# Infini-attention and a Fourier mixer on one core: three steps of the woven stage later in SyncE's order, and one pair of row loads into other buffers

## The chip, the cores and the metric

The kernel runs on one core of one Trainium2 chip. Its engines are TensorE (PE in the profile), VectorE (DVE), ScalarE (ACT), GpSimd (POOL) and SyncE (SP), which here does nothing but issue DMAs. The metric is device time in microseconds (us), lower is better, as the median of several runs.

## What is computed

Two independent layers, whose outputs are joined along the features. A is attention with a compressive memory: 2048 tokens, 576 features, 32 heads of 18, four segments of 512. B is a discrete Fourier transform over the features and then over the tokens, real part only.

```python
def _A_ref(x, wq, wk, wv, wo, beta):
    # q, k, v: x @ w, split into 32 heads of 18 and N = 4 segments of L = 512
    for s in range(N):
        qs, ks, vs = q[:, :, s], k[:, :, s], v[:, :, s]
        logits = jnp.einsum("bhqd,bhkd->bhqk", qs, ks) * scale + mask
        p = _softmax(logits, axis=-1)
        a_dot = jnp.einsum("bhqk,bhkd->bhqd", p, vs)
        pq = phi(qs)
        num = jnp.einsum("bhld,bhde->bhle", pq, M)
        den = jnp.einsum("bhld,bhd->bhl", pq, z)[..., None] + 1e-6
        outs.append(g * (num / den) + (1.0 - g) * a_dot)
        M = M + jnp.einsum("bhld,bhle->bhde", phi(ks), vs)
        z = z + jnp.einsum("bhld->bhd", phi(ks))
    return o @ wo                                   # o: outs, heads joined again

def _B_ref(x, dft_seq_re, dft_seq_im, dft_hid_re, dft_hid_im):
    a = jnp.einsum("bsd,ed->bse", x, dft_hid_re)
    b = jnp.einsum("bsd,ed->bse", x, dft_hid_im)
    return jnp.einsum("ts,bse->bte", dft_seq_re, a) - jnp.einsum("ts,bse->bte", dft_seq_im, b)
```

Everything is float32; the kernel splits operands into a high and a low part and adds up products of the parts.

## The kernel before

**Three stages.** The first projects q, k and v segment by segment, looks up the memory, and leaves q and k (`qd`, `kd`, as bf16 pieces in six slots of a row), the values (`vd`) and the memory's part of the output (`amd`) in DRAM. The second, here called the woven stage, runs the softmax attention of all heads and both passes of B at once. The third, the output stage, multiplies the attention output (`od` in DRAM) with `wo`.

**The weave.** `attention()` is a generator over head pairs p = 0 to 67, with eight slots a pair. The main loop takes one slot, calls `tick()`, and then takes pieces of `dense()`, the work of B, until B has had its share. Each engine runs its own instructions in the order in which they are written down by this walk, and SP issues its DMAs in that order too. `later(n, f)` puts f off to the n-th tick from now, so eight ticks are one pair. A step due at a tick is written down before the pieces of `dense()` that follow the slot.

**What attention loads.** Four heads form a group G, so a group is two pairs. `stack_load(G)` puts two DMAs off by one and two ticks: the group's rows of `kd` into `ks_bufs`, and of `qd` into `qs_bufs`; there are four such buffers. Group 0 is loaded in the first stage, group 1 at p = 0, group (p + 3) // 2 in slot 5 of every odd p, so the third group (G = 2) at p = 1. Its first scores are computed in slot 1 of p = 4. `value_load(G)` loads the values of a group into one of two `vst` buffers; the first product with group 0's values (`pv`) comes in slot 2 of p = 4. `copy_parts(s, n)` copies some pieces of q or k rows from one slot of `qd` or `kd` to another, which the stacks of the later groups read; the copies for segment 2, n = 8 to 15, are written down at the odd pairs 1 to 15, those of segment 3 at the even pairs from 4. They serve groups from G = 20 on.

**Maxima.** In slot 4 of an odd p, `maxima(G)` (L1015 to L1018, four small operations on POOL) cuts the row maxima of a group; in slot 1 of the next pair `maxima_transpose` (L1022) transposes them on PE, ACT copies them (L1024), and one tick later two small DMAs `qs<-mt` put them into the stack.

**What B loads.** B works through a list of tiles, `CHUNKS`. For the first pass these are 16 tiles of the transposed input (`xtT`, 320 KB) and then tiles of the sequence matrix (`cT`, 256 KB). `c_load(n)` loads tile n into one of four `craw` buffers; `hidden(0, n)` asks for tile n + 4 when it begins, and in its middle has tile n + 2 cut (`c_cut`): ACT makes the high part (L451, L453), POOL the low part one tick later (L456, L458). `hidden` itself is L628 to L634. The tiles 0 to 4 are loaded in the first stage.

**Output stage.** Sixteen token tiles are worked on as eight pairs (n, n + 8) in steps n = 0 to 7. A step has seven products (`p1` to `p7`), of which `p4` and `p3` belong to the pair before; they end in the stores of that pair. `left(n + 1)` prepares the next pair from its rows during step n: POOL and DVE add and subtract, ACT and DVE cut (L833 to L853). `o_load` loads the rows of a token tile from `od`, 320 KB. Pair 0 goes into `qs3`/`ks3`, pair 1 into one buffer each of the tags `phi` and `plo` (two buffers each, used by attention until its end), pairs 2 and 3 into the four `craw` buffers at the end of B, and pairs 4 to 7 into `craw` again at the start of steps 2 to 5. The intermediate tiles `u` rotate through ten buffers, four a step.

**The last rows.** After the last product of attention, `pv_out`, `turn_out` (L1118: transposed by DVE, then stored to `od`) and `turn_tails` (L1130: DVE transposes the last eight features of four groups, DMA to `odt`, DMA from `odt` twice into the fifth part of `od`) follow one another through `later`; their ticks fall into the steps 0 and 1. The rows of tiles 12 to 15 need them. Before a row load, `while due: tick()` writes down everything that is still put off.

Of the kernel before, what the change touches and what calls it, by code (L numbers as in the profile page):

```python
# [12 lines left out]
F32 = mybir.dt.float32  # L13
# [10 lines left out]
P = 128  # L24
# [16 lines left out]
def infini_attention_and_fnet(ctx: ExitStack, tc: tile.TileContext, xT, wqk, w8, wv, wo, beta, xtT, cT, hT, out):  # L41
# [46 lines left out]
    def later(n, fn, *a):  # L88
        due.setdefault(clock[0] + n, []).append((fn, a))
# [112 lines left out]
    for i in range(2):  # L202
        kn.append(tuple(sk.tile([P, D], F32R, name=f"kn{n}{i}") for n in "hl"))
        t = sk.tile([P, 2, H, 19], F32R, name=f"vn{i}")
# [3 lines left out]
    for i in range(3):  # L208
        t = sb.tile([P, H, 55], BF16, name=f"vs{i}")
# [277 lines left out]
    def stack_load(G):  # L487
        if G < NG:
            s, g8 = divmod(G, 8)
            rows = slice(g8 * 72, g8 * 72 + 72)  # L490
            for n, (buf, src) in enumerate(((ks_bufs, kd), (qs_bufs, qd))):
                later(1 + n, dma, buf[G % 4][:NPAIR], src[s][rows].rearrange("(h d) c t -> (d c) h t", d=DH))

    def value_load(G):
        if G < NG:
            s, g8 = divmod(G, 8)
            VS[G] = sa.tile([P, 4, 220], BF16, name="vst", bufs=2)
            dma(VS[G], vd[s][:, :, g8])

    for s in range(NSEG):  # L500
# [8 lines left out]
        for n, m in enumerate((0, 1, 2, 3, 8, 4, 5, 6, 7)):  # L509
# [12 lines left out]
            if not more and n == 4:  # L522
                p1k.close()
                sr = ctx.enter_context(tc.tile_pool(name="sb2r", bufs=1, side="right", reuse_waits="tile"))
# [39 lines left out]
    def bank(name, shape, dtype, tag):  # L564
        turns[tag] ^= 1
        return ps.tile(shape, dtype, name=name, tag=f"{tag}{turns[tag]}", bufs=1)
# [117 lines left out]
    def o_load(t, tile_of):  # L684
        s, a = divmod(t, 4)
        o = tile_of()
        dma(o, od[s][:, a * P:a * P + P].rearrange("c p x -> p c x"))
        O[t] = o

    def o_pair(n):  # L690
        for t in (n, n + 8):
            o_load(t, lambda: sr.tile([P, 5, P], F32, name="craw", bufs=4))

    PLAN = {}

    def right_operands():
        raw, late = {}, {}

        def at(p, slot, fn, *a):
            PLAN.setdefault(8 * p + slot, []).append((fn, a))  # L700
# [102 lines left out]
        for t in (0, 8):  # L803
            at(66, 4, o_load, t, lambda t=t: sq.tile([P, 4, 256], F32, name="oraw", tag="qs3" if t else "ks3").rearrange(
                "p a x -> p (a x)")[:, :5 * P].rearrange("p (k x) -> p k x", k=5))
        for t, tag in ((1, "phi"), (9, "plo")):
            at(67, 4, o_load, t, lambda tag=tag: sa.tile([P, 5, P], F32, name="oraw", tag=tag, bufs=2))
        prepare = []
        at(67, 2, lambda: prepare.append(left(0)))
        for n in range(6):  # L810
# [45 lines left out]
    def seventh(o, n, x, w, first=False, tail=None):  # L856
        hi, lo = LEFT[n][x]
        terms = []
        for c in range(2):
            wh, wl = WO[w, c]  # L860
            terms += [(hi[:, c], wl), (hi[:, c], wh), (lo[:, c], wh)]
        if tail:
            terms += [(LEFT[n][tail[0]], m) for m in TAIL[tail[1]]]
        for i, (a, b) in enumerate(terms):
            pe.matmul(o, a, b, start=first and i == 0, stop=True, skip_group_check=True)  # L865
# [6 lines left out]
    def output_stage(second):  # L872
        C, Z, U = slice(0, 288), slice(288, 576), {}

        def p1(n):
            u = U[n] = [sb.tile([P, 576], F32, name="u", tag="ab", bufs=10) for _ in range(4)]
            u += [bank("s", [P, L], F32, "s")[:, :288], bank("t", [P, L], F32, "t")[:, :288],
                  ps.tile([P, 288], F32, name="d", bufs=3)]
            seventh(u[4], n, "A11", "B11", True)
            yield  # L880
            act.activation(u[0][:, C], u[4], AF.Copy)

        def p6(n):
            u = U[n]
            seventh(u[5], n, "S2", "T2", True)
            yield
            dve.tensor_tensor(u[0][:, Z], u[5], u[0][:, C], OP.add)

        def p4(n):
            u = U[n]  # L890
            seventh(u[5], n, "A22", "T4", tail=(2, 0))
            yield
            dve.tensor_tensor(u[3][:, C], u[5], u[0][:, C], OP.add)
            store(n + 8, u[3], slice(0, D))

        def p5(n):
            seventh(U[n][6], n, "S1", "T1", True)
            yield

        def p3(n):  # L900
            u = U[n]
            seventh(u[6], n, "S4", "B22", tail=(1, 2))
            yield
            dve.tensor_tensor(u[2][:, Z], u[6], u[0][:, Z], OP.add)
            store(n, u[2], Z if n == 7 else slice(0, D), n == 7)

        def p7(n):
            u = U[n]
            seventh(u[5], n, "S3", "T3", tail=(2, 2))
            yield  # L910
            dve.tensor_tensor(u[1][:, C], u[5], u[0][:, C], OP.add)
            dve.tensor_tensor(u[3][:, Z], u[6], u[1][:, C], OP.add)

        def p2(n):
            u = U[n]
            seventh(u[4], n, "A12", "B21", tail=(1, 1))
            yield
            act.activation(u[2][:, C], u[4], AF.Copy)
            if n == 7:
                store(n, u[2], C)  # L920

        for n in range(8):
            todo = [(p1, n), (p6, n), (p4, n - 1), (p5, n), (p3, n - 1), (p7, n), (p2, n)]
            if n == 7:
                todo += [(p4, n), (p3, n)]
            if 2 <= n < 6:
                while due:
                    tick()
                o_pair(n + 2)
            prepare = second if n == 0 else left(n + 1) if n < 7 else iter(())  # L930
            for fn, k in todo:
                if k < 0:
                    continue
                piece = fn(k)
                next(piece)
                if n:
                    next(prepare, None)
                next(piece, None)
                if n == 0:
                    next(prepare, None)  # L940
                if n == 0 and fn is p5:
                    pv_out(NP - 1)
                tick()
                tick()
            for _ in prepare:
                pass

    sq = ctx.enter_context(tc.tile_pool(name="sb2q", bufs=1, side="right", reuse_waits="tile"))
    sa = ctx.enter_context(tc.tile_pool(name="sb2a", bufs=1, reuse_waits="tile"))
# [195 lines left out]
    def attention():  # L1145
        for p in range(NP + V_LAG):
            def even(lag, fn, *a):
                if 0 <= p - lag < NP:
                    fn(2 * (p - lag), *a)

            def odd(lag, fn, *a):
                if 0 <= p - lag < NP:
                    fn(2 * (p - lag) + 1, *a)

            if p < 2:
                OG.append(sa.tile([P, 4, 72], F32, name=f"og{p}"))
            if p == 0:
                value_load(0)
                stack_load(1)
            if p % 2 == 0:  # L1160
                later(39, value_load, p // 2 + 1)
                later(30, memory_load, p // 2)
            even(T_LAG + 1, t_lo, 0)
            odd(F_LAG + 1, f_exp, 2)
            odd(F_LAG + 1, f_split_hi)
            yield SLOTS[0]
            G = p // 2 - 1 if p % 2 == 0 and 0 < p <= NP else None
            even(0, s_fill, 0)
            even(T_LAG, t_fill, 0)
            even(T_LAG, t_fill, 1, G)  # L1170
            if G is not None and p < T_LAG:
                maxima_transpose(G, bank("trm", [P, L], F32, "t"))
            odd(F_LAG + 1, f_split_lo, pool, 512, 1280)
            yield SLOTS[1]
            even(0, s_fill, 1)
            odd(F_LAG + 1, f_split_lo, dve, 0, 512)
            yield SLOTS[2]
            even(V_LAG, pv)
            if p < 2:
                stacks(sq, p + 2)  # L1180
            even(0, s_fill, 2)
            even(T_LAG, t_mask)
            yield SLOTS[3]
            odd(F_LAG, f_fill, 1)
            even(T_LAG, t_fill, 2)
            odd(F_LAG, f_fill, 0)
            if p % 2 and p < NP:
                maxima(p // 2)
            yield SLOTS[4]
            odd(F_LAG + 1, f_turn)  # L1190
            if p % 2:
                stack_load((p + 3) // 2)
                if p < 16:
                    later(2, copy_parts, 2, 8 + p // 2)
            elif 4 <= p < 36:
                later(2, copy_parts, 3, (p - 4) // 2)
            even(T_LAG, t_hi)
            yield SLOTS[5]
            odd(V_LAG, pv)
            odd(F_LAG, f_fill, 2)  # L1200
            odd(F_LAG, f_exp, 1)
            even(T_LAG, t_lo, 1)
            even(T_LAG, t_lo, 2)
            yield SLOTS[6]
            odd(F_LAG, f_exp, 0)
            if V_LAG <= p < NP + V_LAG - 1:
                pv_out(p - V_LAG)
            yield SLOTS[7]
# [8 lines left out]
    for n, w in enumerate(attention()):  # L1217
# [4 lines left out]
        while td / total_d < ta / total_a:  # L1222
            t = next(d, BREAK)
# [13 lines left out]
    while due:  # L1237
        tick()
    output_stage(prepare)


# [41 lines left out]
```

## Time and profile before

| | |
|---|---|
| Median of 3 runs | 988.99 us (987.43 to 990.12) |
| The profiled execution's own time | 992.54 us |
| Its span in the profile | 990.8 us, mean granted PE clock 0.998 |
| Busy: PE, DVE, ACT, POOL | 980.7, 785.6, 713.9, 676.7 us |
| DMA | 209.97 MB, 212 GB/s in the mean |
| Chain that ended last: PE, DVE, DMA, issue | 92%, 5%, 1%, 1% of the span |
| First stage, woven stage, output stage | to about 218 us, to about 932 us, to the end |

The profile is one execution, recorded by the hardware profiler; times in it count from the start of its span. The rows of a timeline give start, duration, engine, line, operation, tiles written and read, shape, and in brackets the idle time of the engine before them and what ended it. PE loads weights (PEld) beside its products. A DMA's row on SP is its issue, not its transfer.

### The profile page before, as it was taken

The numbers are of one execution on the slowest core, as the hardware profiler recorded it, in microseconds if no ns is written. First come the engines' busy times: TensorE is split into PE (matmuls) and PEld (weight loads), VectorE is DVE, ScalarE is ACT, GpSimd is POOL, SyncE is SP. The second block draws the span as 40 slices with busy tenths as digits, with TensorE's granted clock in tenths as the row PEclk, the third lists the DMA queues.
The fourth block names the chain that finished last, engine by engine and source line by source line (L and its number), as shares of the span: only waits on it lengthen the run. The fifth ranks groups of instructions, "written<-read, shape, count | busy, mean of one in ns | idle before, by whom it ended". The sixth has DMA issues, their size and how long they took to land.

```text
span 990.8 us, 25491 instructions
## 1 busy us (share of the span) xinstructions
PE 980.7 (99%) x9246; PEld 919.5 (93%) x9246; DVE 785.6 (79%) x2113; ACT 713.9 (72%) x1687; POOL 676.7 (68%) x746
## 2 busy tenths in 40 slices
PE   9999999998999999999999999999999999999998
PEld 8989989898999999999999999999999999999998
DVE  6657668593678787887898788788888999999884
ACT  6757576663888777877878788886778877778442
POOL 1657576685676667676775777767677976767561
PEclk9999999999999999999999999999999999999999
DMA  7637556767578898899999988889999999988663
GB/s 229 206 117 242 195 178 242 240 234 217 143 181 206 223 233 238 198 229 241 237 261 212 239 207 194 186 190 227 234 231 251 242 244 238 225 196 189 168 202 110
DMA packets 304351, 209.97 MB, mean 212 GB/s; under 512 B 204992, under 2 KB 259136, under 8 KB 304192
## 3 DMA queue, kind: packets, MB, share of 16 engines
q1 hardware_dynamic: 304000, 208.20, 82.0%
q8 instruction: 72, 1.18, 0.5%
q14 instruction: 55, 0.45, 0.1%
q10 hardware_dynamic: 224, 0.14, 0.1%
HBM read 122.37 MB, written 58.98 MB: 183 GB/s over the span
## 4 chain that ended last, share of the span: by engine, by line
PE 92%; DVE 5%; DMA 1%; issue 1%; POOL 0%; ACT 0%; SPq 0%; POOLq 0%; DVEq 0%
PE d L583 38%; PE s L965 7%; PE v L84 6%; PE qk L84 6%; PE qk L250 6%; PE pv L1083 4%; PE d L628 4%; PE d L629 3%; PE d L630 3%; PE pv L1084 2%; PE t L865 1%; PE m L363 1%; PE t L1039 1%; DVE s L971 1%; PE look L396 1%
## 5 line engine op out<-in xcount | busy, mean ns | idle before, releaser
L971 DVE CUSTOM_DVE_ANT_0 s<-s,causal 128x128 f32<-128x128 f32 (+3 forms) x512 | 248.1, 503 | 94.0 <-PE s L965 82.1
L456 POOL TENSOR_TENSOR clo<-craw,chi 128x512 fp32r<-128x512 f32 x159 | 220.2, 1385 | 88.7 <-ACT chi L451 69.3
L583 PE MATMUL d<-wide,chi 128*128 128x288 f32 x1408 | 261.8, 303 | 0.0
L583 PEld LDWEIGHTS d<-wide,chi 128*128 128x128 f32 x1408 | 210.8, 189 | 2.1 <-issue 0.7
L583 PE MATMUL d<-wide,clo 128*128 128x288 f32 x704 | 173.5, 313 | 0.0
L1005 POOL TENSOR_TENSOR hl<-pf,hl 128x768 f16<-128x768 f32 x64 | 112.9, 1764 | 65.1 <-ACT hl L1001 53.6
L1051 ACT ACTIVATE phi<-t 128x384 f16<-128x384 f32 x128 | 61.7, 482 | 102.2 <-PE t L1048 102.2
L965 PE MATMUL s<-ks,qs 108*128 108x128 bf16 (+3 forms) x512 | 133.4, 304 | 1.2 <-DVE negm L971 0.7
L994 ACT ACTIVATE pf<-s,nb 128x128 f32<-128x128 f32 (+3 forms) x256 | 128.1, 526 | 6.2
L1066 DVE TENSOR_TENSOR plo<-pf,phi 128x384 f16<-128x384 f32 (+1 forms) x128 | 125.3, 979 | 0.0
L583 PE MATMUL d<-ab,chi 128*128 128x288 f32 x640 | 123.3, 302 | 0.0
L583 PEld LDWEIGHTS d<-wide,clo 128*128 128x128 f32 x704 | 117.9, 189 | 1.9 <-issue 0.4
L451 ACT ACTIVATE chi<-craw 128x512 fp32r<-128x512 f32 x160 | 100.1, 626 | 6.5 <-DMA craw<-xtT 5.3
L1052 ACT ACTIVATE pf<-t 128x384 f32<-128x384 f32 (+1 forms) x192 | 99.6, 519 | 6.2 <-PE t L1039 5.9
L583 PEld LDWEIGHTS d<-ab,chi 128*128 128x128 f32 x640 | 97.9, 189 | 0.5
L1001 ACT ACTIVATE hl<-pf 128x768 f16<-128x768 f32 (+1 forms) x128 | 87.4, 730 | 2.0
L583 PE MATMUL d<-ab,clo 128*128 128x288 f32 x320 | 83.1, 309 | 0.0
L628 PE MATMUL d<-wide,chi 128*128 128x288 f32 x256 | 82.0, 320 | 0.0
L630 PE MATMUL d<-wide,clo 128*128 128x288 f32 x256 | 76.2, 298 | 0.0
L629 PE MATMUL d<-wide,chi 128*128 128x288 f32 x256 | 76.2, 298 | 0.0
L1066 POOL TENSOR_TENSOR plo<-pf,phi 128x384 f16<-128x384 f32 x64 | 62.4, 975 | 15.1 <-ACT pf L1052 14.5
L1005 DVE TENSOR_TENSOR hl<-pf,hl 128x512 f16<-128x512 f32 x64 | 66.8, 1044 | 0.0
(285 smaller groups left out, 2523.5 us busy)
## 6 DMA issues: line engine op xcount, KB each, us to landing
craw<-cT SPq DMA_DIRECT2D x128, 256.0 KB
ks<-kd SPq DMA_DIRECT2D x32, 432.0 KB
qs<-qd SPq DMA_DIRECT2D x32, 432.0 KB
craw<-xtT SPq DMA_DIRECT2D x32, 320.0 KB
vd<-vs SPq DMA_DIRECT2D x16, 440.0 KB
vst<-vd SPq DMA_DIRECT2D x32, 220.0 KB
qd<-p SPq DMA_DIRECT2D x16, 384.0 KB
kd<-p SPq DMA_DIRECT2D x16, 384.0 KB
```

What stands on the lines that cost most here:

```text
L84: pe.matmul(o, a, b, start=n == 0, stop=n == len(terms) - 1)
L451: act.activation(hi, raw[:, :4], AF.Copy)
L456: engine.tensor_tensor(lo, raw[:, :4], hi.bitcast(F32), OP.subtract)
L583: pe.matmul(o[h], a, b[:, h * 288:h * 288 + 288], start=start, stop=stop)
L628: pe.matmul(o, xh[:, k], wl[k][:, cs], start=k == 0, stop=False)
L629: pe.matmul(o, xh[:, k], wh[k][:, cs], start=False, stop=False)
L630: pe.matmul(o, xl[:, k], wh[k][:, cs], start=False, stop=False)
L965: pe.matmul(o[:, c:c + w], q[:, i * P:w], k[:, :w], start=True, stop=True)
L971: dve.tensor_tensor_reduce(o[:, c:c + w], o[:, c:c + w], CAUSAL[0][:, L - w:], scale=scale, scalar=-LOWEST, op0=OP.add, op1=OP.min, accum_ ...
L994: act.activation(f[:, FIRST_COL[i]:FIRST_COL[i] + w], o[:, c:c + w], AF.Exp, bias=nb[:, i:i + 1], scale=-1.0)
L1005: engine.tensor_tensor(hl[:, 1, a:b], f[:, a:b], hl[:, 0, a:b], OP.subtract)
L1066: (pool if kind == 2 else dve).tensor_tensor(lo[:, a:b], f[:, a:b], hi[:, a:b], OP.subtract)
```

## The change

Four places are edited.

- `attention`, p = 0: the first value tile, loaded at once before, is put off by 20 ticks.
- `attention`, p = 1: the third group's `stack_load` is put off by 6 ticks (its two DMAs follow one and two ticks after). The other groups' loads stay where they were.
- `attention`, odd p: the copies of segment 2 run at the pairs 3 to 17 instead of 1 to 15, in the same sequence.
- The output stage: `o_pair(1)` now stands for the two loads of pair 1, which are the same as before. Pair 4 is loaded at the start of step 1 instead of step 2, into the second buffers of `phi` and `plo` instead of `craw`; what is put off is written down before it, at step 1. Pairs 5, 6 and 7 are loaded at the steps 3, 4 and 5 as before; pair 5 takes the `craw` buffers of pair 2, pair 6 those of pair 3 and pair 7 those of pair 5.

```diff
     def o_pair(n):
-        for t in (n, n + 8):
-            o_load(t, lambda: sr.tile([P, 5, P], F32, name="craw", bufs=4))
+        for t, tag in ((n, "phi"), (n + 8, "plo")):
+            if n in (1, 4):
+                o_load(t, lambda: sa.tile([P, 5, P], F32, name="oraw", tag=tag, bufs=2))
+            else:
+                o_load(t, lambda: sr.tile([P, 5, P], F32, name="craw", bufs=4))
...
-        for t, tag in ((1, "phi"), (9, "plo")):
-            at(67, 4, o_load, t, lambda tag=tag: sa.tile([P, 5, P], F32, name="oraw", tag=tag, bufs=2))
+        at(67, 4, o_pair, 1)
...
-            if 2 <= n < 6:
+            if n in (1, 3, 4, 5):
                 while due:
                     tick()
-                o_pair(n + 2)
+                o_pair(4 if n == 1 else n + 2)
...
             if p == 0:
-                value_load(0)
                 stack_load(1)
+                later(20, value_load, 0)
...
             if p % 2:
-                stack_load((p + 3) // 2)
-                if p < 16:
-                    later(2, copy_parts, 2, 8 + p // 2)
+                if p == 1:
+                    later(6, stack_load, 2)
+                else:
+                    stack_load((p + 3) // 2)
+                if 2 < p < 18:
+                    later(2, copy_parts, 2, 7 + p // 2)
```

## The prediction, made before the changed kernel was run

> **What bounds the kernel now.** I read the page first: the tensor engine (PE) is busy for nearly the whole span, so only stretches in which it stands still, or runs at a lowered clock, can be won back.
>
> ```profile
> span 990.8 us, 25491 instructions
> ...
> PE 980.7 (99%) x9246; PEld 919.5 (93%) x9246; DVE 785.6 (79%) x2113; ACT 713.9 (72%) x1687; POOL 676.7 (68%) x746
> ```
>
> PE is idle for 990.8 - 980.7 = 10.1 us in all. I then asked for PE's busy time in short windows over the whole span; apart from the start-up and the last store, two places stand out, the entry into the woven stage and the middle of the output stage. (Columns: window, length, busy time and count of PE, weight load, DVE, ACT, POOL, granted clock, DMA share, GB/s.)
>
> ```profile
> 225.00:235.00 10.00, 10.00 (x77) 9.76 (x76) 3.66 (x12) 2.65 (x7) 6.40 (x8) 1.00 0.97 276
> 235.00:240.00 5.00, 2.90 (x22) 2.53 (x20) 0.82 (x2) 2.55 (x7) 1.94 (x4) 1.00 0.88 239
> 240.00:245.00 5.00, 4.24 (x23) 4.10 (x24) 1.12 (x3) 1.39 (x4) 2.55 (x6) 0.69 0.42 123
> 245.00:250.00 5.00, 5.00 (x38) 4.74 (x37) 4.00 (x15) 1.33 (x4) 1.44 (x2) 0.97 0.47 162
> 250.00:260.00 10.00, 10.00 (x79) 9.43 (x79) 6.34 (x20) 8.72 (x24) 7.53 (x8) 1.00 0.17 43
> 935.00:945.00 10.00, 10.00 (x77) 10.00 (x77) 9.79 (x22) 4.31 (x11) 6.77 (x9) 1.00 0.19 68
> 945.00:955.00 10.00, 9.97 (x76) 9.74 (x74) 6.47 (x14) 3.94 (x12) 2.99 (x5) 1.00 0.62 192
> 955.00:960.00 5.00, 4.59 (x34) 4.59 (x35) 4.92 (x10) 3.20 (x8) 4.67 (x6) 1.00 0.73 228
> ```
>
> First place: 2.10 + 0.76 = 2.86 us without work between 235 and 245, and right behind it a granted clock of 0.69 and 0.97, which costs 5 x 0.31 + 5 x 0.03 = 1.70 us more. Together 4.56 us. Note the DMA column: full from 225 to 240, nearly empty (0.17) from 250 to 260. Second place: 0.03 + 0.41 = 0.44 us around 955, with the clock at 1.00.
>
> The timeline shows who ends the first stall; the bracket gives the engine's idle time before the row and what ended it.
>
> ```profile
> 237.07 0.63 ACT L451 ACTIVATE chi<-craw 128x512 fp32r<-128x512 f32 x1 [4.68 <-DMA craw<-xtT]
> ...
> 237.83 1.26 POOL L456 TENSOR_TENSOR clo<-craw,chi 128x512 fp32r<-128x512 f32 x1 [5.80 <-ACT chi L451]
> ...
> 240.50 0.20 POOL L1018 TENSOR_TENSOR mb<-negx,mb 128x8 bf16<-128x8 f32 x1
> ...
> 240.76 0.23 PE L1022 MATMUL trm<-ident,mb 128*128 128x128 bf16 x1 [2.86 <-POOL mb L1018]
> ```
>
> PE waits for the last of POOL's four small `maxima` operations. They are ready to run, but POOL works in order and stands in front of them at the cut of a spectral tile, which waits for ACT, which waits 4.68 us for a load. Counting the cuts, this is tile 5 (from 0) of `CHUNKS`. From its cut to PE's restart 240.76 - 237.07 = 3.69 us pass, all in POOL's and ACT's order. PE was ready at 237.90.
>
> SP's own timeline names what was in the DMA queue:
>
> ```profile
> 225.18 0.64 SPq L498 DMA_DIRECT2D vst<-vd  x1
> 225.87 0.70 SPq L94 DMA_DIRECT2D ks<-kd  x1
> 226.66 0.40 SPq L94 DMA_DIRECT2D qs<-qd  x1
> 227.10 2.35 SPq L441 DMA_DIRECT2D craw<-xtT  x3
> 229.50 0.61 SPq L94 DMA_DIRECT2D ks<-kd  x1
> 231.05 0.33 SPq L441 DMA_DIRECT2D craw<-xtT  x1
> 231.43 0.40 SPq L94 DMA_DIRECT2D qs<-qd  x1
> 233.18 2.17 SPq L261 DMA_DIRECT2D qd<-qd  x1
> 241.32 1.68 SPq L94 DMA_DIRECT2D qs<-mt  x2
> 243.10 9.23 SPq L441 DMA_DIRECT2D craw<-xtT  x4
> ...
> 267.03 1.54 SPq L94 DMA_DIRECT2D qs<-mt  x2
> ```
>
> Tile 5 is the first of the three loads at 227.10: 9.97 us from issue to cut. Ahead of it lie the first value tile (220 KB) and the second group's rows (`ks`, `qs`, 432 KB each); behind it the third group's rows (229.50, 231.43) and the first row copy (233.18, 288 KB).
>
> **The first part of the change: three moves in SP's order.** No instruction is added; three steps run at a later tick (8 ticks per head pair). The value tile goes from tick 0 to 20. The third group's two loads go from ticks 14 and 15 to 13 + 6 + 1 = 20 and 21. The first row copy goes from tick 15 to pair 3, and each later copy takes the place of its successor, so one more 144 KB copy runs at pair 17. The first maxima rows (`qs<-mt`) are due at tick 18, so SP's new order is: `mt`, tile 9, value tile, `ks`, `qs`, tile 10. They pass no step that somebody waits for except tile 10.
>
> What tile 5 gains: the traffic counts from tile 4's cut to tile 5's landing.
>
> ```profile
> DMA packets 1715, 2.29 MB, mean 265 GB/s; under 512 B 130, under 2 KB 1292, under 8 KB 1715
> ```
>
> Packets of 512 B to 2 KB: 1292 - 130 = 1162. A stack row is 512 bf16 = 1 KB, so the second group's `ks` and `qs` are 2 x 432 = 864 of them, and the other 298 belong to the third group: some 0.30 MB issued after tile 5 was served before tile 5 was whole. With the value tile's 0.22 MB, 0.52 MB of moved traffic went ahead of it; at 265 GB/s that is 1.96 us. The low end is the value tile alone, 0.22 / 265 = 0.83 us; the high end is the whole stall, 2.86 us. I take 1.96, because the packet count shows later loads being served. Stall left: 2.86 - 1.96 = 0.90 us.
>
> The clock: the trace has 0.44 us of standstill with the clock at 1.00 behind it (955) and 2.86 us with 0.69 behind it. No row lies between, so the 1.70 us may stay or go; 0.90 is nearer to 0.44, so I let them go.
>
> The Trainium skill (TensorE: Matmul & The Clock Gate, Part 1) has the clock halved only after an idle window of about 3.4 us. Here 2.86 us were enough, so the trace does not bear the rule out as an exact bound; by it the 1.70 us would go for any stall that the move leaves.
>
> What the moved loads meet: they land where DMA was at 0.47 and 0.17. 1.08 MB at 265 GB/s is 4.1 us, from about 242 to 247. The third group's first scores and the first value product run around the second `qs<-mt` at 267.03, 20 us later: that work hides them, and without it each late us would be one us of PE. The fourfold load at 243.10 was paced by free buffers over 9.23 us, so three more issues (0.64 + 0.61 + 0.40 us) fit between. The copies feed groups from the 21st on: nothing.
>
> **The second part: the fifth pair's rows.** They are loaded at output step 1, not 2, into the free second buffers of `phi` and `plo`. For this everything still due is ticked out before step 1.
>
> ```profile
> 938.41 0.49 DVE L1118 STREAM_TRANSPOSE ogt<-og 128x128 f32<-128x128 f32 x2
> ...
> 941.91 0.29 DVE L1130 STREAM_TRANSPOSE oglt<-ogl 128x128 f32<-128x128 f32 x1
> ...
> 953.41 0.43 DVE L836 TENSOR_TENSOR ls<-craw 128x256 f32<-128x256 f32 x1 [3.00 <-DMA craw<-od]
> ...
> 955.41 1.07 PE L865 MATMUL t<-late,wide 128*128 128x288 f32 x6 [0.43 <-DVE u L887]
> ```
>
> Between DVE's two transposes and its late subtraction the chain of waits has three DMAs:
>
> ```profile
> 942.44 1.88 DMA odt<-oglt
> ...
> 944.33 5.53 DMA od<-odt
> ...
> 949.93 3.39 DMA craw<-od
> ...
> 954.98 0.38 DVE u L887
> ```
>
> They follow one another; DVE gets the rows 3.00 us late, and PE 0.43 us of that. Ticked out at once, L1130 comes right behind L1118 at 938.9 instead of 941.91, so the first DMA starts at 939.3, some 3.1 us earlier, and the rows land at 953.32 - 3.1 = 950.2, just before DVE wants them (953.41 - 3.00 = 950.41). DVE's small transpose now runs ahead of pair 2's subtractions: 0.29 us, hidden by PE's queue (the windows from 935 to 955 are full but for 0.03 us). Gain 0.43 us; low end 0 (the three DMAs slower by 3 us), high end 0.44.
>
> What is queued behind the new wait: SP stands at the second row load until `od` is written, about 946.8, and the two stores of step 0 stand behind it.
>
> ```profile
> 942.01 0.34 SPq L870 DMA_DIRECT2D out<-u  x1
> ...
> 951.44 0.39 ACT L881 ACTIVATE u<-s 128x288 f32<-128x288 f32 x1
> ```
>
> They then leave at about 947.5 and, with the row load's 3.39 us for a store, are out by 951.5. One of their buffers is written again by ACT at 951.44, and PE needs what follows from it (0.39 + 0.38 us) at 955.41 - 0.43 = 954.98: a cover of 2.7 us, so no cost.
>
> **Sum.** 1.96 + 1.70 + 0.43 = 4.09 us. The profiled execution took 992.54 us, 1.7 us around its span; it would become 988.45. It is 3.55 us above the median of the runs shown (988.99), which has no trace; I carry the gain over whole: 988.99 - 4.09 = **984.9 us**. With all of the stall gone it is 984.0.
>
> **Rivals.**
>
> *Ring order.* Only what is issued before tile 5 delays it, and the 298 later packets went through engines that were already past it. Then only the value tile counts: stall 2.03 us, long enough for the clock to be cut as before. Gain 0.83 + 0.43 = 1.26, **987.7 us**; with the clock kept 2.96, 986.0. For it: tile 4, issued just ahead of the same loads, was cut 3.70 us after its issue.
>
> ```profile
> 224.74 0.39 SPq L441 DMA_DIRECT2D craw<-xtT  x1
> ...
> 228.44 0.63 ACT L451 ACTIVATE chi<-craw 128x512 fp32r<-128x512 f32 x1 [0.24 <-DMA craw<-xtT]
> ```
>
> Against it: the packet count, if an engine can serve out of order. The Trainium skill (DMA: Bandwidth & Descriptors, Queues, rings and completion order) says that each engine takes descriptors in ring order; the count over all engines agrees with it only if they run unevenly.
>
> *Tile 5 late by itself.* The DMA queue is full from 225 on, also with the second group's rows alone, and the unprofiled runs may not have this stall at its full size, as their median lies 3.55 us lower. Then 0.43 us or little more is won: **988.6 us**. This is also the case in which the change does not do what it says.
>
> *The stall moves (slower).* Tile 10 now stands behind 1.08 MB in SP's order as tile 5 did, and POOL's second `maxima` stands behind its cut. If it becomes that late, PE stands at the second transpose and the clock falls: + 4.56, against 0.83 and 0.43 won: **992.3 us**. It decides if tile 10 lands after about 257, where POOL needs it; issued at 243.5, even tile 5's 9.97 us would bring it in at 253.5, and the queue is emptier.
>
> **How the numbers follow.** Forecast 0.58, ring order 0.22, late by itself 0.12, the moved stall 0.08. 0.3% of 988.99 is 2.97 us, about what a measurement can tell from no change: faster means below 986.0. The forecast lies there nearly always (0.56 of 0.58); ring order with the clock kept stands at the limit (0.06). Faster 0.62; same 0.30, from the rest of ring order and the tile late by itself; slower 0.08. The range runs from 983.4 (984.0 less the scatter of runs) to 988.6, where two rivals are inside; the forecast's own range is 983.4 to 986.0.
>
> **What would show it.** Right: ACT's wait before the sixth spectral cut falls from 4.68 to about 2.7 us, PE's wait at L1022 to 0.9 or less, the clock stays at 1.00 from 240 to 250, value tile and third group stand behind `qs<-mt` on SP, and PE has no wait for L887 near 955. Wrong: an L1022 wait near 2 us (ring order), one at the second transpose (moved stall), or a clock cut behind a stall below 1 us. What would make the number wrong with all this right: runs without a profile that never had the 4.56 us.

## The result, and the profile after

Measured side by side, 15 runs each: 987.44 us median (985.89 to 987.96) against 989.38 us before (987.43 to 993.95), ratio 0.9972 with a 95% interval of 0.9961 to 0.9983. By the ratio the change makes the kernel about 2.8 us faster (1.7 to 3.9 us by its interval); the two medians lie 1.94 us apart. That is clear of no change, but less than the 0.3% from which the prediction counted a kernel as faster. The profiled execution took 987.47 us with a span of 985.7 us, against 992.54 and 990.8.

The windows over the two places of the prediction, in the changed kernel (columns as before: length, busy time of PE, weight load, DVE, ACT, POOL, granted clock, DMA share, GB/s):

```profile
225.00:235.00 10.00, 10.00 (x77) 9.76 (x76) 4.12 (x13) 3.78 (x10) 7.52 (x9) 1.00 0.91 297
235.00:240.00 5.00, 5.00 (x40) 4.81 (x38) 1.58 (x4) 1.90 (x6) 3.04 (x8) 1.00 0.02 4
240.00:245.00 5.00, 5.00 (x40) 4.67 (x39) 3.71 (x15) 1.96 (x6) 1.75 (x2) 1.00 0.68 184
245.00:250.00 5.00, 5.00 (x41) 4.74 (x40) 1.69 (x5) 4.22 (x14) 2.47 (x3) 1.00 0.99 293
...
945.00:955.00 10.00, 10.00 (x78) 10.00 (x77) 8.06 (x15) 4.71 (x14) 5.90 (x8) 1.00 0.90 290
955.00:960.00 5.00, 5.00 (x40) 5.00 (x39) 4.32 (x10) 1.36 (x4) 4.18 (x5) 1.00 0.53 170
```

Both stalls and the clock cut are gone; PE is busy throughout. DMA is now idle where it was full (0.02 from 235 to 240) and full where it was idle (0.99 from 245 to 250). The timelines of ACT, POOL and PE show the chain of the first stall again, two lines further down in the code:

```profile
233.00 0.63 ACT L451 ACTIVATE chi<-craw 128x512 fp32r<-128x512 f32 x1 [0.73 <-DMA craw<-xtT]
...
236.47 0.20 POOL L1020 TENSOR_TENSOR mb<-negx,mb 128x8 bf16<-128x8 f32 x1
...
237.62 0.22 PE L1024 MATMUL trm<-ident,mb 128*128 128x128 bf16 x1
```

ACT waits 0.73 us for tile 5 instead of 4.68, and POOL's maxima are ready 0.95 us before PE wants them. SP's timeline has the order that was worked out:

```profile
225.06 0.65 SPq L94 DMA_DIRECT2D ks<-kd  x1
225.80 0.55 SPq L94 DMA_DIRECT2D qs<-qd  x1
226.41 5.08 SPq L441 DMA_DIRECT2D craw<-xtT  x4
238.17 1.69 SPq L94 DMA_DIRECT2D qs<-mt  x2
239.97 0.35 SPq L441 DMA_DIRECT2D craw<-xtT  x1
240.38 0.61 SPq L498 DMA_DIRECT2D vst<-vd  x1
241.04 0.58 SPq L94 DMA_DIRECT2D ks<-kd  x1
241.66 0.45 SPq L94 DMA_DIRECT2D qs<-qd  x1
```

In the output stage DVE transposes the tails right behind the other rows, 0.42 us after them instead of 3.50, and the three DMAs start earlier by as much:

```profile
934.56 0.49 DVE L1120 STREAM_TRANSPOSE ogt<-og 128x128 f32<-128x128 f32 x2
934.98 0.27 DVE L1132 STREAM_TRANSPOSE oglt<-ogl 128x128 f32<-128x128 f32 x1
...
946.46 0.71 DVE L838 TENSOR_TENSOR ls<-oraw 128x256 f32<-128x256 f32 x1
```

DVE's subtraction for pair 4 has no wait in front of it any more. SP stands at the row load from 937.97 on and issues the two stores of step 0 behind it, together with two more:

```profile
937.97 5.02 SPq L687 DMA_DIRECT2D oraw<-od  x2
943.08 2.43 SPq L872 DMA_DIRECT2D out<-u  x4
```

Nobody waits for that: PE is full from 935 on.

The list of PE's waits (us in total, times, longest) has a new entry, the last, of the kind that wanders from execution to execution (two more profiles of the same kernel, e8_changed and e12_changed below, don't have it):

```profile
PE warm L239 <- DVE ones L68: 1.1, 1, 1.1
PE s L967 <- DVE negm L973: 1.1, 3, 0.4
PE t L1041 <- DMA qs<-mt: 0.8, 1, 0.8
```

### The profile page after: what moved, and what is told of

The parts are those of the page before. It is cut to its first block, busy times and chain, and to the rows that moved or that the text cites. A ratio compares the mean times of both kernels' runs of the same rounds, so it can differ in the third digit from the quotient of the medians.

```text
span 985.7 us, 25490 instructions
## 1 busy us (share of the span) xinstructions
PE 978.7 (99%) x9246; PEld 917.6 (93%) x9246; DVE 786.1 (80%) x2113; ACT 714.3 (72%) x1687; POOL 675.7 (69%) x746
## 4 chain that ended last, share of the span: by engine, by line
PE 94%; DVE 3%; DMA 1%; ACT 1%; issue 1%; POOL 0%; SPq 0%
PE d L583 38%; PE s L967 7%; PE v L84 6%; PE qk L84 6%; PE qk L250 6%; PE pv L1085 4%; PE d L628 3%; PE d L629 3%; PE d L630 3%; PE t L867 2%; PE pv L1086 2%; PE d L867 2%; PE s L867 1%; PE m L363 1%; PE t L1041 1%; PE look L396 1%
```

## The experiments

The kernels ran in three sets, each set on one chip and beside 35 runs of the kernel before, five rounds each. Three theories stood against each other: A, every load in the stretch delays tile 5; B, ring order, only what is issued ahead of it does; C, how late tile 5 is differs from execution to execution, and the profiled one before was a bad one.

### Each edit alone

**e1_rows**: the output stage's hunks of the diff alone.

> The kernel before with the output stage's edit alone (pair 4's rows at step 1). All theories: PE has no wait for L887 in the middle of the output stage any more (0.43 us before), and the three DMAs odt, od, row load start about 3 us earlier; time 0.4 us below before (ratio 0.9996). Entry into the woven stage: theory A (the loads around tile 5 make it late, every time) expects PE's wait at L1022 again near 2.9 us with the clock cut behind it. Theory C (how late tile 5 comes differs from execution to execution, and the profiled one before was a bad one) expects any wait between 0 and 2.9 us here.

Ratio 0.9996 (0.9979 to 1.0013). Wait for L887 gone, DMAs earlier; but the entry stalled less than in the profile of before, although it is the same code there: 2.14 us. Theory C has a first point. PE's clock was cut behind it (windows of e1_rows):

```profile
235.00:240.00 5.00, 2.86 (x20) 2.49 (x19) 1.94 (x5) 2.82 (x8) 3.24 (x7) 0.94 0.89 236
240.00:245.00 5.00, 5.00 (x30) 4.86 (x30) 0.90 (x5) 1.13 (x3) 1.87 (x3) 0.72 0.62 206
```

The cut costs 5 x 0.06 + 5 x 0.28 = 1.70 us, the same as before's.

**e2_value**: the value tile alone.

```diff
-                value_load(0)
                 stack_load(1)
+                later(20, value_load, 0)
```

> The kernel before with the first value tile put off by 20 ticks, nothing else. Theory B (ring order: only what is issued ahead of tile 5 delays it) expects the whole effect of the entry from this alone: ACT waits under 1.5 us for tile 5, PE's wait at L1022 gone or under 0.5 us, clock at 1.00, ratio near 0.998. Theory A (later loads delay it as well) expects only 0.83 us less: ACT's wait near 3.9 us, PE's wait at L1022 near 2 us, ratio 0.999 or nearer to 1.

Ratio 0.9976 (0.9962 to 0.9991): the whole effect of the change, from one line. ACT's timeline in this kernel:

```profile
232.95 0.63 ACT L451 ACTIVATE chi<-craw 128x512 fp32r<-128x512 f32 x1 [0.62 <-DMA craw<-xtT]
```

No wait at L1022, clock at 1.00. In this profile B's expectation is met. A's ratio of 0.999 still lies at the edge of the interval; the same edit once more (e9_value below) excludes it with 0.9974 (0.9962 to 0.9985), but the profile of that run is less clean. The 12 runs lie within 987.18 to 989.44, those of before within 986.94 to 994.34.

**e3_group**: the third group's loads alone.

```diff
-                stack_load((p + 3) // 2)
+                if p == 1:
+                    later(6, stack_load, 2)
+                else:
+                    stack_load((p + 3) // 2)
```

> The kernel before with the third group's two loads put off by 6 ticks, nothing else. Theory A expects tile 5 some 1.1 us earlier (298 packets of 1 KB at 265 GB/s), PE's wait at L1022 near 1.7 us, ratio about 0.998. Theory B expects tile 5 as late as before: PE's wait as in a kernel without this edit, ratio 0.9995 to 1.0005.

Ratio 0.9998 (0.9980 to 1.0015), B's figure. The profile is not B's: tile 5 came earlier than in any other kernel with the value tile in front.

```profile
234.92 0.63 ACT L451 ACTIVATE chi<-craw 128x512 fp32r<-128x512 f32 x1 [2.43 <-DMA craw<-xtT]
```

PE's wait was 0.65 us, the clock stayed. Yet the runs reach from 987.43 to 993.63, as widely as before's, so one profile does not speak for them.

**e4_copies**: the copies one odd pair later.

```diff
-                if p < 16:
-                    later(2, copy_parts, 2, 8 + p // 2)
+                if 2 < p < 18:
+                    later(2, copy_parts, 2, 7 + p // 2)
```

> The kernel before with the row copies of segment 2 one odd pair later, nothing else. Theories A and B: no effect, since the first copy was issued at 233.18, 6 us behind tile 5: PE's wait at L1022 as in before, ratio 0.9995 to 1.0005. Theory C: the wait differs from before's 2.86 us although nothing that precedes tile 5 is changed.

Ratio 1.0004 (0.9985 to 1.0022): nothing, as expected. Its profile is a second point for C: with everything ahead of tile 5 unchanged, PE waited 1.65 us, and here the clock was not cut (windows of e4_copies).

```profile
235.00:240.00 5.00, 3.35 (x26) 2.98 (x25) 1.95 (x5) 2.45 (x7) 2.85 (x7) 1.00 0.82 240
240.00:245.00 5.00, 5.00 (x39) 4.67 (x39) 2.01 (x9) 1.81 (x5) 3.11 (x4) 1.00 0.44 147
```

### What it is about the value tile

**e5_behind**: `later(5, value_load, 0)` instead of 20, so the same load stands behind tile 5, and all else as before.

> The kernel before with the first value tile put off by 5 ticks only, so that it is issued right behind tile 5 and ahead of the third group; the same bytes in the same 3 us. Ring order (B) expects tile 5 as early as in e2_value: ACT's wait for it 0.5 to 0.9 us, no wait at L1022, clock 1.00, ratio 0.997 to 0.998; tile 6 comes later but has some 3 us of cover. If instead the load of the queue as a whole counts (A), tile 5 is late again: ACT's wait 2.4 to 4.7 us, a wait at L1022 of 0.7 to 2.9 us, ratio 0.999 to 1.001.

Ratio 0.9985 (0.9974 to 0.9997). No wait at L1022, clock 1.00; ACT waited 1.59 us for tile 5, above B's 0.5 to 0.9 and below A's 2.4:

```profile
234.22 0.63 ACT L451 ACTIVATE chi<-craw 128x512 fp32r<-128x512 f32 x1 [1.59 <-DMA craw<-xtT]
```

So the place in the order matters, for the same bytes in the same 3 us, though the interval only just excludes 1. The load behind is not simply left for later: from tile 4's cut to this row the DMA view of the run counts 571 packets under 512 B, against 55 in the changed kernel, so some 500 of the value tile's 512 packets were served before tile 5 was whole. The time lies 0.001 above that of the kernels that move the tile far away (the intervals overlap).

**e6_long_runs**: another load of 220 KB in the value tile's place, in four times longer runs. It reads other rows of `vd`; the right ones follow at tick 20.

```diff
-                value_load(0)
+                VS[0] = sa.tile([P, 4, 220], BF16, name="vst", bufs=2)
+                dma(VS[0].rearrange("p a c -> p (a c)"), vd[0][:, 0, 0:4].rearrange("p g c -> p (g c)"))
                 stack_load(1)
+                later(20, dma, VS[0], vd[0][:, :, 0])
```

> The kernel before with a load of the same 220 KB, from the same array into the same tile, at the value tile's place, but in 128 runs of 1760 B (their content isn't used), and the value tile itself put off by 20 ticks. If bytes ahead in the ring count (B1), tile 5 comes 220 KB / 265 GB/s = 0.8 us later than in e2_value: ACT's wait near 1.4 us, no wait at L1022, ratio near 0.998. If 512 runs of 440 B are what makes the queue uneven (B2), the same result; the two differ in e7. If any further load ahead brings the uneven queue (B3), ACT's wait is 2.4 to 4.7 us and the ratio 0.999 to 1.001.

Ratio 0.9995 (0.9984 to 1.0006), ACT's wait 2.50 us, PE's 0.73: the figures of B3, and the interval excludes B1's 0.998. The profile alone would not decide it, since e9_value below has a wait of 2.44 us with no load in this place. By the time of the runs, short runs are not needed for the cost: another load of this size in this place leaves the kernel 0.0020, or 2.0 us, above e8_changed (which has the other moves as well) on the same chip, more than its 0.83 us of bytes. Whether short runs add something of their own is not shown.

**e7_two_tiles**: the second value tile behind the first one, ahead of the second group.

```diff
                 value_load(0)
+                value_load(1)
                 stack_load(1)
...
-                later(39, value_load, p // 2 + 1)
+                if p:
+                    later(39, value_load, p // 2 + 1)
```

> The kernel before with the second value tile loaded right behind the first one, ahead of the second group: the suspected cost doubled. B1 (bytes) expects tile 5 another 0.8 us later than in before: ACT's wait 3.2 to 5.5 us, PE's wait at L1022 1.5 to 3.7 us, ratio 1.001 to 1.002. B2 (the 440 B runs) expects the addition that one tile brought over e2_value, 1.8 to 4 us, once more: ACT's wait 5 to 8 us, PE's wait 3.5 to 6 us with the clock cut, ratio 1.003 to 1.006. A theory by which the value tile is of no matter: ratio 1.000.

Ratio 1.0023 (1.0012 to 1.0035). ACT waited 4.88 us, PE 3.06, the clock fell to 0.66 from 240 to 245. The profile fits B1, the ratio lies just above its range. Between no tile (0.9976, on another chip), one (1) and two (1.0023) the time goes up by some 2.3 us each: the value tile's place has a price that can be dialled in both directions. It is not all lateness of tile 5. All 12 runs of this kernel have a mean granted clock of 0.998 or less, as profiles with a clock cut do, against 4 of the 35 runs of before beside it. At 1.70 us a cut, 31 more in 35 make 1.5 us of the 2.3, and the rest is about the 0.83 us of the tile's bytes.

**e8_changed**: the changed kernel.

> The changed kernel once more, beside the others on one chip. Expected: no wait at L1022, clock 1.00, ratio 0.997 to 0.998, within 0.0005 of e5_behind if ring order holds, since the other three edits then bring nothing.

Ratio 0.9975 (0.9964 to 0.9985), ACT's wait 0.49 us, no wait at L1022. e5_behind is 0.0010 above it, not within 0.0005.

### The four combinations on one chip

**e9_value** has e2_value's edit, **e10_value_rows** that and the output stage's hunks, **e11_entry** the three moves without them, **e12_changed** is the changed kernel.

> The first value tile's move alone, again, on one chip with the next three. If the value tile is the whole effect: ratio 0.9976, as e2_value measured, and the next three within 0.0005 of it.

> The value tile's move and the output stage's edit. Theory R0 (the rows' three DMAs are hidden unless DVE waits for them for more than some 2.6 us, so the edit brings 0 to 0.1 us in the mean): ratio as e9_value within 0.0003. Theory R1 (it brings its 0.43 us and more, in most executions): 0.0004 to 0.001 below e9_value.

> The three moves in SP's order, without the output stage's edit. If the third group's loads and the copies bring nothing once the value tile is out of the way: as e9_value within 0.0003. If they also relieve tiles 5 to 8: ACT's wait for tile 5 lower than in e9_value, and the ratio 0.0005 to 0.001 below it.

> The changed kernel, third time: ratio 0.997 to 0.998, no wait at L1022. With the value tile as the whole effect it equals e9_value within 0.0005; otherwise it is lower by what e10_value_rows and e11_entry show.

| | ratio to before | interval | median, us |
|---|---|---|---|
| e9_value | 0.9974 | 0.9962 to 0.9985 | 987.80 |
| e10_value_rows | 0.9973 | 0.9963 to 0.9983 | 987.61 |
| e11_entry | 0.9972 | 0.9959 to 0.9984 | 987.66 |
| e12_changed | 0.9965 | 0.9954 to 0.9976 | 987.22 |

The value tile is the effect to within 0.0009, and the intervals overlap. R0's figure came out for the rows, but intervals of 0.0010 to either side don't exclude R1; whether the rows and the other moves together are worth half a microsecond or more is not settled by these runs. The profile of e9_value, unlike e2_value's, has a short wait left at the transpose:

```profile
238.16 0.23 PE L1022 MATMUL trm<-ident,mb 128*128 128x128 bf16 x1 [0.66 <-POOL mb L1018]
```

The runs without a profile have their mean granted clock on record. It is 0.997 or 0.998 in the three profiled executions in which the clock was cut at the entry, and 0.999 or 1.000 in all others, so a run at 0.998 or less is counted here as one with a cut. Times are means, in us:

| chip of | runs of before with a cut | their time | the runs without | kernels with the value tile moved |
|---|---|---|---|---|
| e1 to e4 | 15 of 35 | 992.5 | 989.0 | 988.1 (e2_value) |
| e5 to e8 | 4 of 35 | 992.3 | 989.4 | 987.3 (e8_changed) |
| e9 to e12 | 13 of 35 | 992.2 | 989.5 | 987.5 (all four) |

None of the 98 runs on record with the value tile moved, e5_behind's and the changed kernel's first 15 among them, has a cut. Against the last column, the runs of before with a cut lose 4.4 to 5.0 us, stall and cut together, and the others 0.9 to 2.0 us. So theory C holds, 32 of 105 runs are as bad as the profiled one, and these bad runs come with the value tile in front.

All kernels' entries side by side, each from its one profile:

| kernel | value tile | third group | ACT's wait for tile 5 | PE's wait at the transpose | clock, 240 to 245 |
|---|---|---|---|---|---|
| before | ahead | early | 4.68 | 2.86 | 0.69 |
| e1_rows | ahead | early | 3.95 | 2.14 | 0.72 |
| e4_copies | ahead | early | 3.44 | 1.65 | 1.00 |
| e7_two_tiles | two ahead | early | 4.88 | 3.06 | 0.66 |
| e6_long_runs | other load ahead | early | 2.50 | 0.73 | 1.00 |
| e3_group | ahead | late | 2.43 | 0.65 | 1.00 |
| e5_behind | behind tile 5 | early | 1.59 | 0 | 1.00 |
| e2_value, e9_value, e10_value_rows | late | early | 0.62, 2.44, 1.67 | 0, 0.66, 0 | 1.00 |
| changed, e8, e11, e12 | late | late | 0.73, 0.49, 0.33, 1.47 | 0 | 1.00 |

PE's wait follows from ACT's: it is ACT's wait less 1.8 us (4.68 - 2.86, 3.95 - 2.14, 2.43 - 0.65), which is the cover behind tile 5. Means by rows: 4.02 us with all as before, 1.58 without the value tile, 0.76 without the third group either. So theory A may have a point for tile 5 itself: the third group's loads, issued behind it, would cost it some 0.8 us. The single values overlap (0.62 to 2.44 and 0.33 to 1.47), so this is not shown. It would count for little, because with the value tile gone the wait is mostly below the cover. The value tile's step is clearer, 3.44 to 4.68 against 0.62 to 2.44, though e3_group with the tile ahead has 2.43.

## Why the prediction was right, and where it was off

**The place and the mechanism** were right: ACT waits for tile 5, POOL's maxima stand behind its cut, PE behind them; with the tile earlier the stall and the clock cut go. The sum against the profiled execution was 988.45 us and that kernel's profile came to 987.47. The median is another matter. 987.44 us lies inside the stated range, but outside the forecast's own 983.4 to 986.0, and next to ring order's 987.7, although the stall of 2 us and the clock cut that ring order expected are not there. The range held only because it had been widened for the rivals, which is luck as far as the forecast goes.

**The term that was mis-sized** is the first, in its two halves. The value tile was priced at 0.22 MB / 265 GB/s = 0.83 us, the third group at 0.30 / 265 = 1.13 us. By the means above the value tile is worth 4.02 - 1.58 = 2.4 us and the group 0.8, the latter within the scatter. Neither the bytes nor the rate was as assumed. The traffic from tile 4's cut to tile 5's landing, in the changed kernel and in e6_long_runs:

```profile
DMA packets 994, 1.43 MB, mean 322 GB/s; under 512 B 55, under 2 KB 689, under 8 KB 994
```

```profile
DMA packets 1247, 1.72 MB, mean 272 GB/s; under 512 B 65, under 2 KB 921, under 8 KB 1247
```

Before, the row showed 2.29 MB at 265 GB/s. So 0.86 MB less was served in the changed kernel, not 0.52; at 265 GB/s that is 3.2 of the 4.2 us by which the stretch became shorter, and the higher rate is the rest. The rate does not follow from the load in front: the same stretch has 271 and 281 GB/s in e9_value and e10_value_rows, which have none, and 315 in e2_value. It goes with the lateness.

The packet count, too, was read the wrong way round. Packets issued behind tile 5 were served before it was whole in every kernel: of the packets of 2 KB and more, some 423 before and 305 after, tile 5 has 128 (320 KB in pieces of 2,560 B). More of them are served when tile 5 is late, so they are no measure of what made it late. In e6_long_runs the count is 921 - 65 = 856, less than the second group's 864, so none of the third group need have been served, and tile 5 was 2.50 us late all the same.

A term that the sum put at nothing is SP's own time. The issue of the value tile takes 0.64 us on SP, and tile 5 is issued 1.34 us before tile 4's cut in the mean of the three kernels with all as before at the entry, 2.02 us in the three without the value tile. These 0.7 us and the 0.83 us of bytes would make 1.5 of the 2.4 us. How much an earlier issue counts in a full queue was not tried on its own: no run moves the issue without the bytes. So why a load of 220 KB in front costs tile 5 more than its bytes stays open.

**The step that failed** is "I carry the gain over whole". The profiled execution lay 3.55 us above the median shown, and that was part of the stall itself: the same entry gave 2.86, 2.14 and 1.65 us in three profiles, the last without the clock cut. The loss, stall and cut together, was 4.56, 3.84 and 1.65 us, 3.4 in the mean, and what the ratios show (0.0028, 0.0025 and 0.0035 of 989 us: 2.8, 2.5 and 3.5 us) is near that. The clocks of the runs without a profile say it more plainly: 32 of 105 runs of before had the cut, and lost 4.4 to 5.0 us, about the 4.56 of the prediction; the other 73 lost 0.9 to 2.0 us. The gain carried over whole was that of three runs in ten. The forecast for the profile held to 1 us, the one for the median was 2.5 us too low. The rival that a tile late by itself makes the unprofiled runs less bad was half of the truth, as a matter of size.

**The clock**: kept, since no stall is left. For the 0.90 us that was expected to remain the choice would have been right: 0.65, 0.66, 0.73 and 1.65 us left it at 1.00, 2.14 us cut it.

**The rows**: the chain was right in the links that the trace shows. Tails transposed 0.42 us after the rest, rows some 3 us earlier, DVE's wait gone. The 0.43 us belonged to that one execution, the only one of the nine profiled kernels with the old order in which PE waits there: DVE's wait has a cover of 3.00 - 0.43 = 2.57 us before PE notices, and the other kernels with the old order show waits of up to this size (1.8 to 2.7 us) that cost PE nothing. From e2_value, DVE's timeline:

```profile
948.93 0.43 DVE L836 TENSOR_TENSOR ls<-craw 128x256 f32<-128x256 f32 x1 [2.26 <-DMA craw<-od]
```

The cover was in the numbers already, as DVE's wait less PE's, and wasn't worked out.

**The rivals.** Ring order was right that a load ahead costs tile 5 more than the same load behind it (e5_behind against before, at the edge of the interval), and its reading of the packet count, that later packets say nothing of the cause, held up better than the forecast's. It was wrong that a stall of 2 us is left. The stall did not move to tile 10: ACT cuts it at 253.11 without a wait. The copies and the moved loads cost nothing that shows, as said (e4_copies, 0.9985 to 1.0022; no wait for the third group's rows or the value tile in the profile after).

**What the span's 5.1 us consist of**: 2.86 + 1.70 + 0.44 = 5.0 from the two places. PE's other small waits grew by some 0.7 us, among them the new 0.80 at L1041, and about as much was won after PE's last product (4.4 us to the end before, 3.9 after) and in PE's busy time beside the clock cut (980.7 - 1.7 against 978.7).

## What to carry to other kernels

When an in-order engine stalls for a load, look at what was issued ahead of that load and needed last: here a tile wanted 40 us later stood in front, and moving one line brought the gain to within 0.0009. Price such a load by trying it: bytes over the mean rate came out three times too low, and SP's time to issue it was not in them. And a stall read from one profile is one draw: compare the profiled execution's time with the median before carrying its gain over, look at the granted clock of the other runs, and subtract the cover that the waits of two neighbouring engines show.

## What was unexpected in the hardware

PE's clock was cut behind standstills of 2.14, 2.86 and 3.06 us and not behind 0.65, 0.66, 0.73 and 1.65 us. Each cut cost some 1.7 us. The Trainium skill (TensorE: Matmul & The Clock Gate, Part 1) asks for an idle window of about 3.4 us; the trace does not agree: among these seven standstills the cut came from 2.14 us on and not up to 1.65. And a transfer of 220 KB ahead of a queue of 1.2 MB delayed the load behind that queue by 2.4 us in the mean of three profiles each (3.44 to 4.68 us against 0.62 to 2.44), where its bytes at the rate of that stretch make 0.83 us and its issue on SP 0.64.
